# A dilated convolution with a gated activation: another split into six-step and four-step groups, and a new order of all instructions

## The chip, the cores and the metric

The kernel runs on one core of one Trainium2 chip. A core has a matrix engine (PE, with its weight loads PEld), a vector engine (DVE), a scalar engine (ACT), a general engine (POOL, also called GpSimd), a queue engine (SP) and DMA. The engines run side by side, each takes its own instructions strictly in the order in which the program lists them, and they wait for each other by semaphores. The metric is device time in microseconds (us), as a median of several runs.

## The reference: what is computed

`x` has 2 sequences of 16,000 steps with 256 channels; `w` holds three taps of 256 by 512, `w_o` is 256 by 256, all bf16.

```
pad = 4                                  # (K - 1) * dilation, K = 3, dilation 2
xp = pad x with 4 zero steps in front
h = xp[t+4] @ w[0] + xp[t+2] @ w[1] + xp[t] @ w[2]      # B, T, 512
f, g = h[..., :256], h[..., 256:]
z = tanh(f) * sigmoid(g)
return z @ w_o                                           # B, T, 256
```

Three outputs that lie two steps apart share inputs. Done plainly they need nine products of an input by a tap. A fast-convolution scheme of the Toom-Cook kind makes two outputs from four products, or three outputs from five, at the price of sums ahead of the products (over inputs and over weights) and sums behind them (over products).

## The kernel before, in words

**Groups.** The steps of a sequence are cut into groups, named in `GROUPS` (lines 13 to 16). A group of kind A covers `6*R` steps and a group of kind B covers `4*R`; R is 256 unless the word says otherwise. A group of kind P (one, at the very start, `P160`) does the plain three-tap convolution. Channels lie across the 128 partitions and R runs along the free axis, so one product of a group is, for one block of 128 of the 512 outputs, two matmuls (two halves of the 256 input channels) with 2R columns. Before there are 15 groups A, 7 groups B with R = 256, one B160 and one B128.

**Products.** A group has four blocks (`oi` 0 to 3). A block of A has five products, called "first", "mid", "last", "zero" and "inf" (`product`, line 336; tokens F, M, L, Z, I); a block of B has four (no "mid"). They add up in PSUM banks `b` (three buffers) and `a` (two buffers).

**Operands of the products** (`pre` and `operand`, lines 261 to 333). B needs `m`, `p`, `d0`, `d3`, each one sum of two slices of the transposed input `xt`. A needs `u1`, three scaled copies of it (`u3`, `uh`, `ud`), and four sums `rp`, `rm`, `r0`, `ri`, each made out of an `f`, `e`, `u0` or `u2` plus one of those scaled copies. The engine is written in the token: a plain name (`u0.4`) is one DVE instruction over 1,024 elements; a name with `q` (`u0.4q7`) is one of four quarters on POOL, held until the DVE instruction so many places back has finished; a name ending in `d` (`r0.4d`) is an accumulating DMA that POOL issues.

**Behind the products.** Per block: `c` copies bank `b` to `ss` (ACT, line 382); `A` makes the bank `a` start value (DVE, line 388); in A-groups `h` or `k` makes `hh` on DVE or by a copy on ACT (lines 397 and 395) and `Y` makes `yy` (DVE, lines 412 and 414). Then `b`, `y`, `a` are activations on ACT (line 433), three to a block of A and two to a block of B. When two blocks are there, `g` multiplies tanh by sigmoid on DVE (`gate`, line 452), over 1,536 elements for A, 1,024 for B. `P` multiplies 128 rows of z by `w_o` (four matmuls of 256 columns for a pair of steps), `e` or `v` evicts the result to `osb` on ACT or DVE (lines 487 and 479), and `s` stores it from SP (line 496). Loads (`x`) are transposing DMAs on the same SP queue (line 167). The last group's output products are split into a first half (H) and a second half (R).

**Order.** `ORDER` (lines 17 to 21) gives the order of blocks over the whole kernel: four times the group's number, blocks of different groups possibly interleaved. `PLAN` (lines 22 to 72) is a list of all instructions written out by hand or by a planner; each token is emitted in turn, so PLAN fixes the order on every engine and queue, and which of two engines does an `h`/`k`, an `e`/`v` or an operand. Before, groups 8, 9 and 10 (B) come first, and from then on blocks of a B-group stand between blocks of the A-groups ("1 11 1 1 1 11 2 2 2 11").

**Buffers.** `SLOTS` (line 139) says how many buffers each ring has; `osb`, the evicted outputs, has 3.

Of the kernel before, what the change touches and what calls it, by code (L numbers as in the profile page):

```python
# [26 lines left out]
m.3 L e6 F d3.3 b wa.9q1 s3 P A c x F e7 uh.1 M p.3 I k0 g Z c I e.2 a L ud.1 b P f.1q1 A a L x wa.13q47 e8 F Y
wa.11q35 P c A f.1q18 Z y g M wa.15q20 b Z h1 I b u1.2 F a L x u0.2 c I ud.2 e9 F A f.1q1 a M Y P c P k2 u3.1 s4
u2.1 M e10 rm.1d L u1.3 e11 ri.1d Z k3 A I r0.1d b L u3.2 a Y F f.3q10 y P A c Z uh.2 I f.1q16 Y b L y rm.2d u2.2 F
a I f.2 c Z A P a rp.1 M b P y g Z k4 F g e12 e.3q1 L c I s6 A b x P e.3q38 e14 M Y a F m.4q45 h5 I c e.3q32 v13 Z y  # L30
L d3.4q13 v15 b M m.4q10 A P k6 d3.4q7 F Y a L ri.2d u0.3 c Z y A I b P u3.3 f.3q1 Y L a F e16 rp.2d ud.3 Z g c
r0.2d I p.4 b M a A P k7 F u1.4 Z c uh.3 L g b r0.3d M e17 I d0.4q20 A k8 F s8 P Y x f.3q3 c L v19 a d0.4q61 M y Z A
d3.4q27 I h9 b u0.4q53 P y Y u0.4q90 F a L v20 m.4q26 c I A e.3q75 Z e18 s5 Y L a m.4q61 I b g f.3q61 Z y F A b P y
rm.3d u2.3 P c F rp.3d f.4 a Z u2.4 M rp.4d c P g b ri.3d M k10 u3.4 F e21 h11 L u1.5q1 e22 I A c P u1.5q19 a L Y
e23 P d3.4q44 A y M s10 d0.4q13 Y Z e24 s9 u1.5q2 I x b uh.4 I d0.4q48 e25 h12 Z a F g u1.5q1 b L c P Y u0.4q27 y F
A L a P f.5 c Z y A M b u3.5 I x e.4 k13 Z a F ud.4 uh.5 b L u2.5 I c F g e26 M c u1.6q85 P A k14 P u1.6q8 a Y M
rm.4d e27 L v28 e29 I u0.4q7 A s12 k15 P s11 Z ud.5 a u1.6q10 Y L b P u1.6q96 A e30 Z ri.4d y f.6 I s13 b x F Y P a
d0.5 F c p.5 Z e32 L c u0.5 I b u3.6 M A y P k16 r0.4 F a Z v31 e.6q1 c L g I b r0.5d M e33 e.6q17 A F k17 s14 P
u0.6 c s7 d3.5q2 P s1 a Y L e34 d3.5q60 M A y Z e.6q4 I y Y rp.5d P k18 e.5 I b g Z rm.5d a L b u2.6q120 v35 F a P A
c F d3.5q26 e36 Y P d3.5q39 L c g u2.6q62 Z y A P b M ri.5d m.5 e37 Z rp.6d h19 e38 F y e.7 I c L uh.6 I b g r0.6d M  # L40
a u1.7q26 P a h20 F e39 A P u1.7q79 e40 s16 L Y c u2.6q109 s15 P A x Z e.6q71 e42 Y I u1.7q23 b M v41 y u2.7q41 Z
h21 a F u2.6q63 I b g u1.7q4 L c F a Y L c u2.7q64 P A y P rm.6d uh.7 y M A I k22 v44 Z a u3.7 Z ud.6 b L u0.7 e43
ri.6d P ud.7 b F A e45 I u1.8q83 F c Y s18 P a u1.8q154 x M c g u1.8q133 I y M h23 e46 P a f.7q145 h24 Z L g b P
f.8q159 e47 A L e48 x u2.7q23 F Y I Y u1.8q180 c Z a A f.8q125 P b L u2.7q4 e49 Z s19 A f.8q109 F s17 b u3.8 I r0.7d
c u0.8 Z rm.7d a F e.8 b P u2.8 rm.8d c M y F f.7q117 h25 P c ri.7d M g e50 L y I A p.6q1 k26 M Y a P f.7q192 I h27
y f.7q191 L e51 Z f.8q112 A a L p.6q21 b P Y P e52 rp.7d Y F y f.9q107 A Z c I v54 b Z u1.9q53 e53 P m.6 a F ud.8 L
c e.9q0 P A y P rp.8d e55 g M b I s22 h28 Z x a F uh.8 b u2.9 L c P A e.9q1 e56 F Y M f.9q104 c I h29 e57 u1.9q43 I
a M g p.6q6 a L k30 x Z A P u1.9q84 b Y L e58 f.9q114 I v59 y Z u1.9q98 A a F e.9q4 P b Y P c r0.8d ud.9 s23 F e60
u3.9 ri.8d Z g c L d0.6 b I y A M F uh.9 e.10q65 P h31 c Z g a u1.10q5 L y M A b I u1.10q36 Y P e61 F e62 e.10q32
h32 Z a v63 e.9q32 L c I f.9q200 b A M u1.10q16 a Y P y u1.10q39 F h33 Z rp.9d c g L b rm.9d I Y y L ri.9d a A F P  # L50
e64 f.10 Z c s25 u0.9 P s24 b I A s20 r0.9d e65 F u0.10 y M uh.10 c Z u3.10 a P d3.6 M k34 g I b e.11q87 L e66 h35 F
a P A u1.11q32 c L e67 rp.10d Y P M p.6q105 A e69 Z k36 Y r0.10d P b v68 I u2.10q75 y Z v70 a I g u2.10q30 L s27 b
s26 F A x F u2.10q9 c P Y a u1.11q9 P c L u1.11q19 y Z A e.10q142 e71 I ud.10 P b u1.11q8 v72 M e73 u2.10q29 F h37 y
Z e.10q118 c x I g e.11q73 a L M b Y P k38 rm.10d P A e74 L ri.10d u0.11 a F y Z A u1.12q66 c P Y I b M e75 u2.11 Z
a h39 P b f.11 F e76 L g c rp.11d F I m.7q7 A c L a Y d0.7q34 P e77 m.7q16 M A u1.12q14 e78 I s30 h40 Z p.7q33 x a
ud.11 Z b u2.12 L y P d0.7q0 A b I f.12q23 Y F y d3.7q56 F uh.11 c Z g r0.11d c M s29 y p.7q137 P h41 a M d3.7q22
v79 b I e.11q96 L k42 u1.12q12 F a A L u1.12q16 c Y P p.7q33 I A y e.11q62 Z a Y P b L u3.11 e80 Z g rm.11d F e81
uh.12 P ud.12 c u1.13q106 A P y M ri.11d v83 b I d3.7q10 h43 e82 Z a F e.12 s32 m.7q30 L b s31 P c f.12q57 Y F e84
u1.13q96 A M c I u1.13q53 h44 y P p.7q65 e85 M g u1.13q123 a Z L h45 b I f.12q30 A F a f.12q73 Y L c I A rp.12d y Z
Y a d3.7q72 L I b A Z y uh.13 F b u3.12 Z g c rm.12d I a F u0.12 b M g e86 P r0.12d k46 F m.7q16 v87 P c L u1.14 c  # L60
d0.7q12 M e88 A P d0.7q6 a P ri.12d Y k47 M ud.13 e89 L e.13 k48 u0.13q1 Z s34 A e90 s21 I b x P uh.14 u0.13q18 Y a
L F y g u2.13q1 P y A I c Z f.13q10 e91 Y s28 P u0.13q13 b s33 L Z a f.14 u2.13q8 F b A P c ud.14 Z u3.13 F y g M
rm.13d c I m.8q1 b h49 M e92 F u0.13q1 a h50 s35 L e93 f.13q11 I A c P f.13q23 L e94 Y u2.13q20 M e95 Y Z p.8q9 a
h51 e.14q53 P b I A u2.13q19 e96 L y f.13q26 F s37 Y Z a u0.14q15 I b A P rp.13d c F a rp.14d L c Z ri.13d A I r0.13
b Z y M u3.14 v97 F b e.14q1 a P h52 I u2.14q14 y F c g e.14q54 L e98 P Y c M e99 d3.8q30 A P e.14q96 y M h53 s38 P
u0.14q25 e100 Z k54 g u0.14q6 L a I b A P e101 u2.14q78 Y L a F u0.14q31 y P A I c Y d3.8q1 Z a P v102 b Z g y s39 L
# [570 lines left out]
```

## Time and profile before

| what | value |
|---|---|
| median of 3 runs | 262.25 us (261.99 to 262.55) |
| the profiled execution's own time | 262.04 us |
| its span, first to last instruction | 260.3 us |
| granted PE clock | 0.999 |
| PE, DVE, ACT, POOL busy | 253.9, 242.7, 242.9, 170.8 us |

"Busy" is the union of an engine's instructions in time. Instructions of one engine overlap at their ends: a matmul of 512 columns is shown with 379 ns, but the next one can start much earlier. What an engine needs for one instruction is therefore read from the distance between the starts of two that follow without a wait, and busy time is an upper bound of it.

### The profile page before, as it was taken

The page shows a single profiled execution, that of the slowest core. Times are in us where ns is not written, and L with a number is a line of the kernel's source. Part 1 is how long each engine was busy: PE and PEld are TensorE (multiplying, and loading weights), DVE is VectorE, ACT ScalarE, POOL GpSimd, SP SyncE. Part 2 cuts the span into 40 slices and gives each one's busy share as a digit, 9 for nine tenths or more (in the row PEclk, how much of TensorE's full clock was granted, in tenths as well). Part 3 has the DMA queues.
Part 4 walks back from the last instruction along what each step waited for, and adds up shares of the span by engine and source line. Part 5 has one row for each costly group of instructions (what it writes and reads, how often), then busy time and mean ns, then how long its engine had stood idle before and what let it go on. Part 6 is the DMA issues. An engine that isn't in the chain of part 4 may idle for free.

```text
span 260.3 us, 4591 instructions
## 1 busy us (share of the span) xinstructions
PE 253.9 (98%) x1468; PEld 142.0 (55%) x1468; DVE 242.7 (93%) x398; ACT 242.9 (93%) x490; POOL 170.8 (66%) x248
## 2 busy tenths in 40 slices
...
GB/s 198 187 208 213 243 214 204 225 229 123 202 212 263 227 221 222 170 242 200 255 186 184 229 128 256 218 236 150 207 164 78 165 236 136 159 101 42 123 161 171
DMA packets 83583, 49.38 MB, mean 190 GB/s; under 512 B 69064, under 2 KB 70344, under 8 KB 83560
## 3 DMA queue, kind: packets, MB, share of 16 engines
...
q10 hardware_dynamic: 912, 0.95, 1.1%
...
q14 instruction: 12, 0.10, 0.1%
...
## 4 chain that ended last, share of the span: by engine, by line
PE 79%; DVE 13%; issue 2%; DMA 2%; ACT 2%; ACTq 1%; POOL 1%; DVEq 0%
PE b L351 46%; PE o_ps L470 18%; PE a L351 12%; DVE a L385 4%; DVE zz L452 2%; DVE yy L385 2%; DMA e<-u 2%; DVE u L330 1%; PE b L371 1%; PE a L371 1%; DVE hh L385 1%; DVE uh L328 1%; ACTq L189 1%; POOL wu L233 1%; DVE d L330 1%
## 5 line engine op out<-in xcount | busy, mean ns | idle before, releaser
L470 PE MATMUL o_ps<-wo_sb,zz 128*128 128x256 bf16 x496 | 71.9, 273 | 0.1
L385 DVE SCALAR_TENSOR_TENSOR a<-ss,b 128x512 f32<-128x512 f32 (+1 forms) x96 | 64.0, 668 | 5.8 <-PE b L351 4.5
L470 PEld LDWEIGHTS <-zz 128*128 128x128 bf16 x496 | 48.4, 98 | 26.6 <-DVE zz L452 0.9
L382 ACT COPY ss<-b 128x512 f32<-128x512 f32 (+1 forms) x96 | 56.1, 591 | 5.2 <-PE b L351 4.4
L487 ACT CAST osb<-o_ps 128x512 bf16<-128x512 f32 x96 | 57.6, 617 | 0.9 <-PE o_ps L470 0.4
L351 PEld LDWEIGHTS <-w_sb 128*128 128x128 bf16 x384 | 37.4, 98 | 38.5 <-issue 2.3
L330 POOL TENSOR_TENSOR u<-xt 128x256 bf16<-128x256 bf16 x68 | 50.5, 757 | 6.1 <-PE b L351 4.7
L452 DVE TENSOR_TENSOR zz<-th,sg 128x1536 bf16<-128x1536 bf16 (+2 forms) x50 | 44.6, 893 | 1.2 <-ACT sg L433 1.2
L351 PE MATMUL b<-f,wp_sb 128*128 128x512 bf16 x120 | 35.7, 379 | 0.4 <-DVE hh L385 0.4
L351 PE MATMUL b<-e,wm_sb 128*128 128x512 bf16 x120 | 35.7, 379 | 0.2 <-DMA e<-u 0.2
L351 PE MATMUL b<-u,w_sb 128*128 128x512 bf16 x120 | 35.7, 379 | 0.2 <-DVE yy L385 0.2
L351 PE MATMUL a<-u,w_sb 128*128 128x512 bf16 x120 | 35.5, 379 | 0.1
L351 PE MATMUL b<-u,wa_sb 128*128 128x512 bf16 x120 | 35.5, 379 | 0.0
L433 ACT ACTIVATE sg<-a 128x512 bf16<-128x512 f32 (+2 forms) x48 | 29.3, 610 | 0.9 <-PE a L351 0.7
L433 ACT ACTIVATE th<-b 128x512 bf16<-128x512 f32 (+2 forms) x48 | 28.8, 601 | 1.2 <-PE b L351 0.9
L433 ACT ACTIVATE th<-a 128x512 bf16<-128x512 f32 (+2 forms) x48 | 29.2, 611 | 0.1
L433 ACT ACTIVATE sg<-b 128x512 bf16<-128x512 f32 (+2 forms) x48 | 28.8, 600 | 0.5 <-PE b L351 0.2
L351 PEld LDWEIGHTS <-wp_sb 128*128 128x128 bf16 x192 | 18.8, 98 | 18.2 <-issue 1.7
L330 POOL TENSOR_TENSOR e<-xt 128x256 bf16<-128x256 bf16 x24 | 19.7, 823 | 12.2 <-PE b L351 6.7
L351 PEld LDWEIGHTS <-wm_sb 128*128 128x128 bf16 x192 | 18.6, 98 | 14.9 <-DMA e<-u 0.7
L330 POOL TENSOR_TENSOR f<-xt 128x256 bf16<-128x256 bf16 x28 | 21.5, 773 | 6.4 <-DVE ud L328 2.8
L385 DVE SCALAR_TENSOR_TENSOR hh<-ss,b 128x512 f32<-128x512 f32 x34 | 23.0, 678 | 0.5 <-PE b L351 0.2
...
## 6 DMA issues: line engine op xcount, KB each, us to landing
...
out_dram<-osb SPq DMA_DIRECT2D x17, 256.0 KB, 3.3
f<-u POOLq DMA_DIRECT2D x14, 256.0 KB, 4.2
e<-u POOLq DMA_DIRECT2D x14, 256.0 KB, 4.1
u<-ud POOLq DMA_DIRECT2D x14, 256.0 KB, 5.6
u<-uh POOLq DMA_DIRECT2D x13, 256.0 KB, 4.7
w_sb<-in_w_dram ACTq DMA_DIRECT2D x3, 256.0 KB, 3.7
xt<-in_x_dram SPq DMA_TRANSPOSE x24, 6.6
```

The source lines that it names most:

```text
L189: return nc.scalar.dma_start(out=w_taps[tap][:], in_=w[tap].rearrange("(ct c) d -> c ct d", c=P))
L233: return nc.gpsimd.tensor_tensor(out=dst[:, d], in0=wu_sb[0][ct][:, d], in1=wu_sb[1 + add][ct][:, d], op=ALU.add)
L328: ins = eng.tensor_scalar_mul(o, a, factor)
L330: ins = eng.tensor_tensor(out=o, in0=a, in1=b, op=op)
L351: nc.tensor.matmul(G[bank, oi][:, :2 * R], lhsT=wmat[:, ct, osl], rhs=G[mv][:, :, ct, :R], start=which == "first" and ct == 0, stop=ct == ...
L371: nc.tensor.matmul(G[bank, oi][:, :4 * r].rearrange("p (j r) -> p j r", j=4), lhsT=w_taps[tap][:, ct, osl], rhs=xt[:, j0:j0 + 4, ct, c0 + ...
L382: nc.scalar.copy(out=G["ss", oi][:, :n], in_=G["b", oi][:, :n])
L385: return note(nc.vector.scalar_tensor_tensor(out=out, in0=in0, scalar=scalar, in1=in1, op0=ALU.mult, op1=op))
L433: nc.scalar.activation(out=G[name, dt][:, j:j + 2, :R], in_=G[bank, oi][:, :2 * R].rearrange("p (q r) -> p q r", q=2), func=(ACT.Tanh, ACT ...
L452: note(nc.vector.tensor_tensor(out=G["z"][:, dt, :, :n], in0=G["th", dt][:, :, :n], in1=G["sg", dt][:, :, :n], op=ALU.mult))
L470: nc.tensor.matmul(o_ps[:, q, :], lhsT=z, rhs=wo_sb[:, dt, :], start=dt == 0 and (q == 0 or len(dts) == NT), stop=dt == NT - 1, skip_group ...
L487: copy(out=G["osb", at][:, 2 * jp:2 * jp + 2, :], in_=o_ps[:])
```

## The change

GROUPS becomes 18 groups A, 3 groups B with R = 256 and one B160 (the B128 goes); the P160 stays. ORDER then lists whole groups one after the other: B-groups 9, 10, 11, then A-groups 1 to 8 and 12 to 21, then 22 (B160). The ring `osb` gets 4 buffers. PLAN is another list for these groups. By tokens, before and after:

| token | before | after |
|---|---|---|
| F, L, Z, I (each, blocks) | 96 | 88 |
| M, Y, y (each, blocks of A) | 60 | 72 |
| c, A, a, b (each) | 96 | 88 |
| h on DVE / k on ACT | 34 / 26 | 41 / 31 |
| g over 1,536 / 1,024 / 512 elements | 30 / 14 / 2 | 36 / 6 / 0 |
| v on DVE / e on ACT | 29 / 97 | 22 / 104 |
| P and H (pieces of output products) | 124 + 2 | 123 + 3 |
| u3, uh, ud on DVE (each) | 15 | 18 |
| m, p, d0, d3 on DVE (together) | 24 | 13 |
| u0, u1, u2, e, f on DVE (together) | 45 | 54 |
| rp, rm, r0, ri on DVE (together) | 5 | 4 |
| rp, rm, r0, ri as DMA (together) | 55 | 67 |
| quarters on POOL, beside 16 for weights | 168 | 160 |
| loads x (beside the first four) / stores s | 20 / 49 | 18 / 46 |

```diff
 GROUPS = (
-    "P160 A A A A A A A B B B B B128",
-    "A A A A A A A A B B B B160",
+    "P160 A A A A A A A A B B B",
+    "A A A A A A A A A A B160",
 )
 ORDER = """
-8 8 8 8 9 9 9 9 10 10 10 10 1 11 1 1 1 11 2 2 2 11 2 3 3 11 3 3 4 21 4 4 4 21 5 5 5 21 5 6 6 21 6 6 7 22 7 7 7 22 13
-13 13 22 13 14 14 22 14 14 15 23 15 15 15 23 16 16 16 23 16 17 17 23 17 17 18 24 18 18 18 24 19 19 19 24 19 20 20 24
-20 20 12 12 12 12
+9 9 9 9 10 10 10 10 11 11 11 11 1 1 1 1 2 2 2 2 3 3 3 3 4 4 4 4 5 5 5 5 6 6 6 6 7 7 7 7 8 8 8 8 12 12 12 12 13 13 13
+13 14 14 14 14 15 15 15 15 16 16 16 16 17 17 17 17 18 18 18 18 19 19 19 19 20 20 20 20 21 21 21 21 22 22 22 22
 """
 PLAN = """
-p.0 m.0 d0.0 d3.0 F D c D D G w L d F wa.6q3 A F c p.1 Z c I G b L d3.1 wa.7q1 a L A P wa.0q8 A x F wa.2q9 I d0.1 c
...
-v118 a P e119 Z P e120 P b s46 e121 P g s45 v122 H e123 H R R s47 v124 e125 s48
+d3.0 m.0 d0.0 p.0 F D c G F w D L c wa.4q3 F A wa.7q5 L c wa.2q5 D A I wa.6q2 d Z m.1 a Z p.1 b L b G I wa.14q1 F A
...
+s41 P e117 v118 I a Z v119 a P b g P s42 e120 g P H v121 H e122 R H v123 R s43 R e124 s44 v125 s45
 """
...
-    SLOTS = {"m": 2, ..., "th": 2, "osb": 3, "odd": 3}
+    SLOTS = {"m": 2, ..., "th": 2, "osb": 4, "odd": 3}
```

More of the change, by code (lines that the diff above doesn't have):

```diff
@@ L27 @@
[L27 to L66, printed above, removed]
@@ new lines @@
+F d3.1 c x P a d0.1 Z L u2.0 b I A c F a u1.0 L c Z g wa.3q1 I b A P wa.0q14 e0 x F f.0 a L ud.0 c wa.11q1 Z A P
+wa.8q11 b I g rp.0d L e1 m.2 Z ri.0d e2 a F e.0 b P A I c s0 d3.2 F e3 Z a u3.0 P u1.1 b rm.0d I p.2 c L a ud.1 P A
+e4 F wa.15q1 e5 L u2.1 wa.10q9 s2 Z c x A I wa.5q29 b L d0.2 a F g wa.12q1 I c A Z a wa.1q35 L u0.0 wa.13q25 b Z A I
+b wa.9q14 F uh.0 a I g r0.0d c F f.1 a Z u1.2 P c L b u0.1 M e6 A F k0 s3 P u3.1 c e.1 Z L e.2 b rm.1d I A e7
+u0.2q40 P a F Y ri.1d e8 M uh.1 c Z s4 g r0.1d I k1 x u3.2 M b g L y ud.2 F u0.2q1 k2 A P c P rp.1 u0.2q15 e9 M Y a
@@ new lines @@
+L u1.3q26 h3 e10 Z y I u1.3q24 A L b u0.2q4 Y P a u1.3q2 F Y y Z u1.3q41 A c I b rm.2d uh.2 Z x u2.2 a M b u3.3 F
+ud.3 k4 I f.2 F c g L rp.2d y M c ri.2d A P k5 r0.2d M Y a L k6 f.3 P e11 Z A x y L e.3 I b Y P e12 F g a I e13
+u1.4q47 Z A c P b uh.3 u1.4q44 M Y a P u0.3q56 v14 k7 Z y F rm.3d e.4 L b g P c f.4q48 F y A I c M f.4q57 Y e15 M
+u1.4q69 h8 a Z e16 h9 u0.3q10 L b I f.4q15 A e17 L u1.4q70 Y y F s8 u0.3q48 I a Y Z c u0.3q25 A P y rp.3d u0.4 M b Z
+u2.3 k10 F ud.4 a ri.3d L u2.4 b I r0.3d A c P y F uh.4 Y M a P e18 h11 e.5q40 Z c g L e.5q3 e19 M e20 Y I k12 s9
@@ new lines @@
+f.4q1 P A b L ri.4d g a Z rp.4d y F u3.4 P b A rm.4d P c f.5 r0.4d F e21 Y M y I u1.5 c Z u2.5q30 h13 a I b M uh.5
+u3.5 a L u2.5q1 h14 F e22 e.5q58 A P e23 L u1.6q4 c Y s10 P e24 A u1.6q100 M y Z h15 e.6q28 y I Y b u1.6q105 P L a g
+e.6q45 F e25 Z Y e26 I c u2.5q4 A s11 P b x g M y Z k16 ud.5 F u0.5 a P L c u0.6 I e27 A M b u2.6q79 P x e28 h17
+u1.6q43 F y Y P u2.6q100 a L v29 c r0.5d P g e30 Z rp.5d e31 P Y e.5q70 M b A P y s12 F h18 e32 u2.5q66 I c u3.6 s13
+Z ri.5d a rm.5 x L b f.6 M y I Y e.7q109 F k19 A P a e.6q104 L c uh.6 Z e33 A f.7q65 I b e.6q82 M Y y F e.7q39 h20 a
@@ new lines @@
+Z rm.6d g c I L b u2.7q43 v34 M a F A y u2.6q70 P k21 Y u2.6q15 P e35 L u1.7 u2.7q131 c Z A e36 I b f.7q75 M Y P a
+f.7q77 h22 F y rp.6d Z ud.6 s14 c ud.7 P r0.6d b g L ri.6d y I Y e37 F A a P M c u3.7 Z y h23 e.8q77 M b g I e.8q44
+k24 L e39 v38 F a L e.8q57 Y s15 c P x e.8q16 A P y A e.7q98 M e40 Z e41 f.7q62 h25 I b Y e.7q15 P a F f.8 u2.7q15 y
+L c P Y u0.8q49 e42 M A e43 rm.7d Z uh.7 k26 P rp.7d u0.7 b I u1.8 L e44 r0.7d F a g s17 Z s16 c I u3.8 b P A a M
+u2.8 e45 F ud.8 k27 P u2.7q1 Y P c u1.9 L y u0.8q46 P y A Z e46 ri.7d M Y b I rp.8d g k28 Z rm.8d a F f.9 b L e.9 I
@@ new lines @@
+c F e47 A u2.9q111 M c s18 P Y u0.9q15 e48 x M h29 y u0.8q162 Z h30 a P u0.9q175 b L uh.8 L y g F e49 I Y c
+u1.10q112 P A a u0.8q79 M y A Z u0.9q148 k31 I Y u0.9q23 b I ud.9 y L r0.8d u3.9 F a uh.9 rm.9d Z v50 c P u1.10q190
+A b s19 P e51 x M Y a f.10q177 F h32 e52 Z u1.10q10 P c g u2.9q102 L b M e53 Y P y u2.9q51 A F y I u1.10q130 h33 c Z
+e.10 r0.9d L b ri.8 M a F rp.9 k34 I u1.11q137 A c L a Y u1.11q17 M e54 A u2.9q16 Z k35 P uh.10 f.10q167 b x Y I y F
+ri.9d g a Z c L g I b f.11q155 P e55 A F e56 u2.10 f.10q96 M a s21 P Y c s20 P u1.11q148 h36 y M e57 ud.10 Z u3.10
@@ new lines @@
+k37 L u0.10 rm.10d b I A L u1.11q2 e58 F Y a P y f.10q113 A Z c I u0.11 rp.10d b M Y r0.10d a F h38 ri.10d y Z c I g
+L b M u3.11 y u1.12q1 A F a P Y f.11q76 e59 I h39 c u1.12q54 Z s22 a x e.11 f.11q199 L e60 P A b M u1.12q124 e61 Y P
+y f.11q134 F h40 Z e62 rp.11d uh.11 L c ud.11 I e.12 b M e63 A u2.12q28 P s6 k41 Y F s23 u2.12q205 a L g rm.11d y Z
+c P u2.12q208 A I e64 u0.12 M b u1.12q26 P e65 Y F y r0.11d u2.11 s24 Z k42 P u3.12 ri.11d c uh.12 P f.12 a L b g M
+rp.12d e66 I u1.13q58 v67 F k43 P a A L u1.13q135 c Y P y u2.12q72 M A e68 e.13q221 Z e69 h44 P rm.12d b Y I
@@ new lines @@
+u1.13q42 e70 F v71 a Z g u1.13q162 c s26 L s25 b I A x M y Y F a P u2.13 k45 Z c ud.12 L u3.13 y ri.12d M A b P
+e.13q31 h46 e72 I F e73 Y u0.13q186 L a g e.13q202 Z c P y A M b P e.13q201 Y k47 I r0.12d uh.13 e74 F ud.13 a
+rm.13d L u1.14 s27 Z c f.13 P y A M rp.13d b P y Y u0.13q195 I e75 h48 F a Z f.14 c L u3.14 b I g P e76 u2.14q38 F y
+Y M c u2.14q126 A P e77 M e.14q144 h49 e78 Z s28 h50 u0.13q44 a s7 L x b e.14q40 I A L e79 u0.13q37 Y F a u2.14q265
+P Y c Z e.14q239 y A M ri.13d b ud.14 I g k51 Z r0.13d a F rp.14d e.15 P c L v80 e81 I uh.14 f.15q209 b M A y P
@@ new lines @@
+r0.15d u2.16 e94 L b P A f.17q56 P y F Y y f.17q8 P c h60 e.16q162 Z a g M rp.16d b L e.17q29 e95 h61 I y F A s34
+d0.3q36 L a Y e.16q94 P c I A f.17q3 y M Y a rm.16d Z e96 h62 I b Z g L b F uh.16 e97 Y P r0.16d c F A P c ud.16 M
+u0.17 a ri.16d I e98 h63 M p.3q3 y Z s35 h64 e99 L e.17q10 P b A d3.3q94 L a u2.17q62 Y F e101 f.17q252 P v100 c Z
+u2.17q62 e102 Y I e.17q4 b A M y P e.17q79 h65 a F rm.17d g Z c L y I d3.3q0 A b M p.3q27 Y a P rp.17d F e103 h66 Z
+c uh.17 I g b r0.17d L a M u2.17q13 Y e104 F h67 y P s37 d0.3q61 P y A s36 L c ud.17 p.3q1 P e105 Y Z d3.3q75 y A
```

17 lines of the change are left out of this document (9 added, 8 removed).

## The prediction

> **What bounds the kernel now.** I read the page first (busy time, chain), then the table of 10 us stretches, then the order of time in one stretch, then the groups by form.
>
> ```profile
> PE 253.9 (98%) x1468; PEld 142.0 (55%) x1468; DVE 242.7 (93%) x398; ACT 242.9 (93%) x490; POOL 170.8 (66%) x248
> ...
> PE 79%; DVE 13%; issue 2%; DMA 2%; ACT 2%; ACTq 1%; POOL 1%; DVEq 0%
> ```
> ```profile
> 0.00:10.00 10.00, 9.03 (x68) 5.71 (x69) 5.41 (x8) 6.80 (x14) 0.81 (x8) 1.00 0.87 193
> 10.00:20.00 10.00, 10.00 (x56) 5.31 (x55) 9.08 (x18) 8.17 (x19) 2.13 (x4) 1.00 1.05 197
> 20.00:30.00 10.00, 10.00 (x55) 5.21 (x54) 10.00 (x19) 8.94 (x20) 5.64 (x9) 1.00 1.16 235
> 30.00:40.00 10.00, 9.78 (x54) 5.01 (x52) 9.80 (x18) 9.44 (x20) 5.69 (x9) 1.00 1.10 212
> 40.00:50.00 10.00, 9.98 (x52) 4.97 (x51) 10.00 (x18) 9.80 (x21) 6.08 (x9) 1.00 1.11 208
> 50.00:60.00 10.00, 9.97 (x57) 5.26 (x55) 9.89 (x17) 9.52 (x19) 6.72 (x10) 1.00 0.99 217
> 90.00:100.00 10.00, 10.00 (x58) 5.35 (x57) 9.96 (x17) 10.00 (x22) 5.43 (x8) 1.00 1.12 264
> 240.00:250.00 10.00, 10.00 (x71) 6.84 (x70) 9.57 (x18) 9.55 (x22) 0.00 (x0) 1.00 0.29 111
> 250.00:260.00 10.00, 5.97 (x55) 5.09 (x53) 4.72 (x10) 6.02 (x14) 0.00 (x0) 0.99 0.49 186
> ```
> ```profile
> 59.57 0.68 DVE L385 SCALAR_TENSOR_TENSOR yy<-hh,a 128x512 f32<-128x512 f32 x1
> 59.94 0.59 PE L351 MATMUL b<-u,wa_sb 128*128 128x512 bf16 x2
> 60.17 0.42 DVE L328 TENSOR_SCALAR ud<-u 128x1024 bf16<-128x1024 bf16 x1
> 60.37 0.59 PE L351 MATMUL b<-u,w_sb 128*128 128x512 bf16 x2
> 61.69 0.60 PE L470 MATMUL o_ps<-wo_sb,zz 128*128 128x256 bf16 x4
> 62.13 0.59 PE L351 MATMUL b<-u,wa_sb 128*128 128x512 bf16 x2
> 63.25 0.95 DVE L452 TENSOR_TENSOR zz<-th,sg 128x1536 bf16<-128x1536 bf16 x1
> ```
> ```profile
> 4.84 2.62 PE b L371 x18
> ...
> 253.78 2.20 PE o_ps L470 x20
> 256.00 0.59 ACT osb L487
> ```
>
> The chain runs on PE for 79%. Columns of the stretches: length, then busy us (and instructions) of PE, PEld, DVE, ACT, POOL, then clock, DMA share, GB/s. Since a busy PE says little, I take distances of starts: two matmuls of 512 columns take 0.43 us (59.94 to 60.37), 0.215 each, four of 256 take 0.44 (61.69 to 62.13), 0.11 each. PE's need is 824 matmuls of 512 columns (15 x 40 + 7 x 32), 177.2 us; 80 of 320 columns (B160 and P160) at 0.134 by proportion, 10.8; and 532 of 256 (500 output products, 32 of B128), 58.5. Sum 246.5. From the first real product at 4.84 to the last at 253.78 + 2.20 = 255.98 are 251.1 us. So PE loses only 4.6 us to everything else. PE binds in every stage.
>
> But DVE and ACT are close behind: between 20 and 60 us DVE is busy 39.69 of 40 us, and PE hardly stops.
>
> **The change part by part.** *PE.* Three groups A more (3 x 40 matmuls of 512), four B less (4 x 32), one B128 less (32 of 256): 8 x 0.215 + 32 x 0.11 = 5.2 us less. Output products are 500 in both. That is the gain offered: 3 x 1,536 outputs from 120 matmuls in place of 144 equivalents.
>
> *DVE and ACT.* Their prices:
>
> ```profile
> L385 DVE SCALAR_TENSOR_TENSOR a<-ss,b 128x512 f32<-128x512 f32 x88 | 60.3, 687 | 4.3 <-PE b L351 3.2 <-ACT hh L395 0.3 <-ACT sg L433 0.2
> L487 ACT CAST osb<-o_ps 128x512 bf16<-128x512 f32 x96 | 57.6, 617 | 0.9 <-PE o_ps L470 0.4
> L382 ACT COPY ss<-b 128x512 f32<-128x512 f32 x88 | 53.0, 608 | 4.8 <-PE b L351 3.9 <-ACT th L433 0.2
> L330 POOL TENSOR_TENSOR u<-xt 128x256 bf16<-128x256 bf16 x68 | 50.5, 757 | 6.1 <-PE b L351 4.7 <-DVE yy L385 0.3 <-DVE hh L385 0.2
> L452 DVE TENSOR_TENSOR zz<-th,sg 128x1536 bf16<-128x1536 bf16 x30 | 32.1, 1073 | 0.0
> L433 ACT ACTIVATE th<-a 128x512 bf16<-128x512 f32 x44 | 27.4, 626 | 0.1
> L433 ACT ACTIVATE sg<-yy 128x512 bf16<-128x512 f32 x30 | 19.6, 653 | 0.3 <-DVE yy L385 0.2
> L330 DVE TENSOR_TENSOR u<-xt 128x1024 bf16<-128x1024 bf16 x28 | 19.3, 701 | 0.0
> L479 DVE CAST osb<-o_ps 128x512 bf16<-128x512 f32 x28 | 18.7, 680 | 0.2 <-PE o_ps L470 0.2
> L351 PEld LDWEIGHTS <-wm_sb 128*128 128x128 bf16 x192 | 18.6, 98 | 14.9 <-DMA e<-u 0.7 <-ACT ss L382 0.6 <-issue 0.2
> L325 POOL DMA_DIRECT2D u<-ud x14 | 16.1, 1148 | 2.0 <-DVE ud L328 2.0
> L452 DVE TENSOR_TENSOR zz<-th,sg 128x1024 bf16<-128x1024 bf16 x14 | 10.0, 711 | 0.0
> L328 DVE TENSOR_SCALAR uh<-u 128x1024 bf16<-128x1024 bf16 x15 | 7.5, 500 | 0.0
> L328 DVE TENSOR_SCALAR ud<-u 128x1024 bf16<-128x1024 bf16 x15 | 6.6, 437 | 0.0
> L328 DVE TENSOR_SCALAR u<-u 128x1024 bf16<-128x1024 bf16 x15 | 6.5, 431 | 0.0
> L385 DVE SCALAR_TENSOR_TENSOR a<-ss,b 128x256 f32<-128x256 f32 x4 | 1.7, 425 | 0.4 <-PE b L351 0.3
> ```
>
> DVE loses 4 full `a` sums (4 x 0.687 = 2.75) and 4 half-wide (4 x 0.425 = 1.70), 8 gates of 1,024 (x 0.711 = 5.69) and 2 of 512 (some 0.4 each, 0.8), 7 evictions (x 0.680 = 4.76), and of the operand sums 13 (11 of m, p, d0, d3, one of them half-wide, and 2 of r0; 0.701 each, 8.8): 24.5 us. It gains 7 `hh` and 12 `yy` (same instruction as the `a` sum, 19 x 0.687 = 13.05), 6 gates of 1,536 (x 1.073 = 6.44), 10 operand sums (4 u1, 1 u0, 1 e, 3 f, 1 rp; 7.0) and 3 each of uh, ud, u3 (3 x 1.368 = 4.10): 30.6 us. Net +6.1 us.
> ACT loses 4 `ss` copies (2.43) and 4 half-wide (0.62 of the full price by the two `a` rows, 1.51), 8 full activations (5.0) and 8 half-wide (3.1): 12.0. It gains 12 activations of `yy` (7.84), 5 `hh` copies (3.04), 7 evictions (4.32): 15.2. Net +3.2 us. So ACT stands at 246.1 busy, DVE at 248.8.
>
> *What of this is on the path.* PE alone would end 5.2 us earlier: span 260.3 - 5.2 = 255.1. DVE has to fit. In the first 20 us it is busy 5.41 + 9.08 = 14.5, in the last 20.3 us 9.57 + 4.72 = 14.3; start and tail keep their shape. Between them lie 220 us with 242.7 - 28.8 = 213.9 busy, 6.1 idle. After: 213.9 + 6.1 = 220.0 us busy in a middle that PE would like to be 214.8 long. By busy time DVE becomes the bound: 40.3 + 220.0 = 260.3, no gain at all. But busy time overstates: the `yy` of 59.57 lasts 0.68 and is followed at 60.17, so an instruction needs 0.08 less than it shows wherever it is followed at once. Nothing in the profile separates overlapped tails from true need, so bounds: below, 0.08 comes off each of the 398 instructions, whose durations, from the first row of this table (60.3) to the smallest, sum to 270.1: need 238.3; above, the 242.7 themselves. Less its ends, the middle needs 209 to 213.9 now and 215 to 220 after, without a single wait.
> DVE's waits: now 6.1 us; in the stage 20 to 60, where DVE sets the pace, 0.31 of 40 (0.8%), 1.7 us over the middle. With the latter the upper need gives 40.3 + 220.0 + 1.7 = 262.0. The other end is PE's 255.1. Neither row is nearer; I take the middle, 258.5: the gain of 5.2 is offered, some 3.4 is given back to DVE and ACT, which are both full from 20 us on, where before B blocks between A blocks gave them rest.
>
> One rule of the skill speaks against the change. Row first: a gate of 1,536 took 0.95 us at 63.25 and 1.073 in the mean, and `uh` 0.500 where `u3` of the same shape took 0.431. The Trainium skill, "SBUF — State Buffer", section "Who interferes with whom", says that a DVE instruction with two SBUF inputs and a GpSimd one that reads SBUF exclude each other for the whole instruction. The trace agrees in kind. By that rule six more gates and three more `uh` at 0.12 and 0.07 would be 0.9 us, and the sum 0.9 later, were the mean prices above not to hold it already.
>
> *POOL.* 8 quarters fewer (8 x 0.757 = 6.1) and 12 accumulating DMAs more (12 x 1.148 = 13.8 at the dearest row): +7.7, 178 of about 259 us, off the path; behind each stand the next operand's quarters, which are wanted several us later. Lower end 0, upper end 7.7 if POOL were the bound, which its 66% excludes; I take 0.
> *SP.* Two loads and three stores fewer on the queue, the same bytes: 0. The fourth `osb` buffer: evictions wait only for PE (row L487, 0.9 us in all), so it brings 0 to 0.9, I take 0.
> *Start.* B-groups first, as before, and the same 16 weight quarters: 0, within 1 us either way.
> *Tail.* The last group is B160 in place of B128: activations, gate and one more half-wide eviction. Between 0 and 1.2 us (two more instructions of about 0.6, row 256.00); I take 0.3.
>
> Sum: span 258.5 + 0.3 = 258.8; 1.74 around it (262.04 own time against 260.3) gives 260.5 against 262.04; the median before stands 0.2 above that run: about 260.6. I forecast 260.5, 0.7% faster.
>
> **The rivals.**
> *PE stays the bound.* For it: 20 to 60 us, DVE 99% busy and PE not stopping. Against it: there ACT was at 94%, now both are full. Time: 255.1 + 0.3 + 1.95 = 257.4.
> *DVE and ACT pass their waits on (slower).* Place: the long run of A-groups from about 30 to 225 us, with no B block between. Engines that take instructions in order cannot catch up once all three are full; each wait of DVE for bank `b` (3.2 us on the `a` row) then lengthens the kernel. At the upper need with today's 6.1 us of waits: 40.3 + 220.0 + 6.1 + 0.3 + 1.95 = 268.7; at the lower need 263.7. It decides once need and waits of the middle exceed 220.3 us: then the time is above 262.8.
> *Late DMAs (slower).* Each A-group hangs on its four accumulating DMAs. They grow from 55 to 67 and lie denser:
>
> ```profile
> u<-ud POOLq DMA_DIRECT2D x14, 256.0 KB, 5.6
> ```
> An A-group moves 0.79 MB in, 0.79 out and 4 x 0.26 by accumulation, 2.6 MB in some 11.5 us: 229 GB/s, against 264 carried at 90 to 100 us. So it should fit. If it doesn't, PE waits as it did once for `e` (0.7 us in all, PEld row): 0.3 to 0.7 us in each of 18 groups, 263 to 270.
>
> **How the numbers follow.** A change under 0.2% (0.5 us) can't be told from none. PE stays the bound, about 257.4: 0.15. Gain partly given back, 258 to 261.7 with 260.5 the likeliest: 0.40. Given back wholly, 261.7 to 262.8: 0.12. Waits passed on, 263 to 268: 0.25. Late DMAs: 0.08. So faster 0.55, same 0.12, slower 0.33. The range reaches from PE's floor, 257.0, to 265.0, which leaves out the upper part of the two slow cases; the likeliest one's own range is 257.4 to 262.
>
> **What would show it.** Right: 1,428 matmuls; DVE busy near 248 and ACT near 246 with the span at 258 to 259; stretches from 30 to 220 us with DVE and ACT both at 9.9 or more; DVE's and ACT's share of the chain far above 13% and 2%. PE then shows less than 10.00 in many stretches. PE's rival: PE's share of the chain stays near 80%. The slow rival: DVE's waits for `b` or for ACT stay at 6 us or grow. The DMA rival: PE or PEld waits on `e`, `f` or `u` by DMA, and landings well above 5.6 us. The prediction is wrong most easily where the need of DVE for an instruction differs from my middle of two bounds, or where POOL's and DVE's exclusion grows in the dense stage.

## The result, and the profile after

| kernel | median (range), executions | ratio to the kernel before, with its 95% interval |
|---|---|---|
| before, first series | 262.19 us (261.99 to 262.55) | 1 |
| after, first series | 259.94 us (259.83 to 263.96), 4 | 0.9907 (0.9893 to 0.9921) |
| before, second series | 262.33 us (261.57 to 262.99), 24 | 1 |
| after, second series (the first experiment) | 260.45 us (259.7 to 265.3), 12 | 0.9945 (0.9914 to 0.9976) |

The ratios compare mean times and leave out executions more than 1.5% above the fastest of the same kernel, so for a kernel that scatters they differ from the ratios of the medians. The changed kernel is faster by 0.5 to 0.9%; 260.5 us was forecast. But its executions fall into two groups, which those of the kernel before do not: 7 of 12 took 259.7 to 260.8 us and 5 took 262.4 to 265.3. Both profiles taken of it are of long ones (263.96 and 263.39 us), so I read them for what lengthens these, and read the short ones from a kernel that differs only in the place of one load ("load later", below; 259.82 us, span 258.0).

Engine row and three stretches of the profile after (columns as before):

```profile
PE 251.0 (96%) x1428; PEld 138.6 (53%) x1428; DVE 244.4 (93%) x404; ACT 244.1 (93%) x490; POOL 179.1 (68%) x252
```
```profile
60.00:70.00 10.00, 7.70 (x42) 3.75 (x41) 7.63 (x14) 7.89 (x16) 6.22 (x10) 1.00 1.24 155
...
150.00:160.00 10.00, 10.00 (x59) 5.48 (x57) 10.00 (x17) 10.00 (x22) 9.39 (x13) 1.00 1.11 236
...
190.00:200.00 10.00, 8.62 (x48) 4.41 (x46) 9.91 (x15) 8.86 (x18) 7.50 (x11) 1.00 1.06 218
```

All 40 matmuls are gone (1,428). At 150 us PE, DVE and ACT are all three busy for the whole stretch. PE loses most of its time in two places: from 60 us on, where all engines are idle for part of the stretch (for want of a DMA, as the next rows show), and at 190 to 200 us, where DVE stays busy and PE waits for it. The waits of the same profile, with total, count and longest:

```profile
PE b L351 <- DMA u<-uh: 2.1, 2, 1.9
...
PEld L351 <- DMA f<-u: 1.6, 2, 0.9
...
PE b L351 <- DVE hh L385: 1.3, 2, 1.2
```

Below, "gaps" is one number for a whole profile: the distances between the starts of successive matmuls less the time of their columns (0.215 us for 512, 0.11 for 256), added up over all matmuls from 4 us on. It is 4.5 us before, 10.6 in the profile after.

### The profile page after: what moved, and what is told of

It is laid out like the page before. It is cut to its first block, busy times and chain, and to the rows that moved or that the text cites. A ratio compares the mean times of both kernels' runs of the same rounds, so it can differ in the third digit from the quotient of the medians.

```text
span 262.1 us, 4570 instructions
## 1 busy us (share of the span) xinstructions
PE 251.0 (96%) x1428; PEld 138.6 (53%) x1428; DVE 244.4 (93%) x404; ACT 244.1 (93%) x490; POOL 179.1 (68%) x252
## 4 chain that ended last, share of the span: by engine, by line
PE 53%; DVE 9%; issue 3%; ACT 1%; DVEq 0%
PE b L351 32%; PE o_ps L470 13%; PE a L351 8%; DVE a L385 2%; DVE yy L385 2%; DVE zz L452 1%; DVE hh L385 1%; DVE osb L479 1%; DVE f L330 1%; DVE u L330 1%; ACT th L433 0%; DVE ud L328 0%; DVE uh L328 0%; DVE u L328 0%; ACT ss L382 0%
## 5 line engine op out<-in xcount | busy, mean ns | idle before, releaser
L330 POOL TENSOR_TENSOR u<-xt 128x256 bf16<-128x256 bf16 x84 | 62.4, 757 | 15.2 <-PE a L351 5.3
L351 PE MATMUL b<-u,w_sb 128*128 128x512 bf16 x144 | 42.8, 379 | 2.7 <-DMA u<-uh 2.1
L351 PE MATMUL b<-f,wp_sb 128*128 128x512 bf16 x144 | 42.7, 379 | 2.2 <-DVE hh L385 1.3
L351 PE MATMUL b<-u,wa_sb 128*128 128x512 bf16 x144 | 42.8, 379 | 0.0
L351 PE MATMUL b<-e,wm_sb 128*128 128x512 bf16 x144 | 42.7, 379 | 0.0
L433 ACT ACTIVATE th<-b 128x512 bf16<-128x512 f32 (+1 forms) x44 | 28.0, 637 | 2.3 <-PE b L351 2.0
L433 ACT ACTIVATE sg<-b 128x512 bf16<-128x512 f32 (+1 forms) x44 | 28.0, 636 | 1.5 <-PE b L351 1.4
L433 ACT ACTIVATE sg<-a 128x512 bf16<-128x512 f32 (+1 forms) x44 | 27.7, 631 | 0.8 <-PE a L351 0.7
L433 ACT ACTIVATE th<-a 128x512 bf16<-128x512 f32 (+1 forms) x44 | 28.1, 639 | 0.1
L385 DVE SCALAR_TENSOR_TENSOR yy<-hh,b 128x512 f32<-128x512 f32 x41 | 27.6, 678 | 0.5 <-PE b L351 0.3
```

Source lines behind the costliest of these rows:

```text
L330: ins = eng.tensor_tensor(out=o, in0=a, in1=b, op=op)
L351: nc.tensor.matmul(G[bank, oi][:, :2 * R], lhsT=wmat[:, ct, osl], rhs=G[mv][:, :, ct, :R], start=which == "first" and ct == 0, stop=ct == ...
L385: return note(nc.vector.scalar_tensor_tensor(out=out, in0=in0, scalar=scalar, in1=in1, op0=ALU.mult, op1=op))
L433: nc.scalar.activation(out=G[name, dt][:, j:j + 2, :R], in_=G[bank, oi][:, :2 * R].rearrange("p (q r) -> p q r", q=2), func=(ACT.Tanh, ACT ...
```

## The experiments

**The changed kernel again.** No edit.

> The changed kernel once more, unaltered, for an undisturbed profile. Theory A (three engines full: PE, DVE and ACT share the loss): 259.9 us, PE's matmul starts show 6 to 7.5 us of gaps between 5 us and the end, most of them behind DVE or ACT, DVE busy near 248. Theory B (PE alone is still the bound and the missing 2.9 us of the 5.2 are lost to late accumulating DMAs): 259.9 us, PE or its weight loads wait 2 us or more on e, f or u by DMA.

Measured: the second series of the table. In its order of time (start, length, what, and in brackets what was waited for), the load at 47.71 us and the DMAs behind it:

```profile
47.71 20.12 SPq L167 DMA_TRANSPOSE xt<-in_x_dram  x2
...
49.24 0.86 POOL L325 DMA_DIRECT2D f<-u  x1 [2.09 <-DVE f L330]
49.78 1.21 POOL L325 DMA_DIRECT2D u<-ud  x1
50.31 1.56 POOL L325 DMA_DIRECT2D u<-uh  x1
...
63.89 0.59 PE L351 MATMUL b<-u,w_sb 128*128 128x512 bf16 x2 [1.50 <-DMA u<-uh]
```
Two of its stretches of 2.5 us:
```profile
52.50:55.00 2.50, 2.50 (x17) 1.47 (x16) 2.50 (x5) 2.50 (x7) 1.09 (x1) 1.00 1.36 119
...
62.50:65.00 2.50, 1.11 (x8) 0.74 (x9) 2.50 (x6) 1.33 (x3) 1.42 (x3) 1.00 1.26 84
```
and its DMA groups from 45 to 70 us (the last number is the median from issue to landing):
```profile
u<-uh POOLq DMA_DIRECT2D x2, 256.0 KB, 12.0
...
xt<-in_x_dram SPq DMA_TRANSPOSE x3, 13.4
```

The two loads shown as one row of 20.12 us are the second and third of three in a row. The third begins at 53.0 us, some 3 us behind three accumulating DMAs, and takes 14.8 us on its queue. Meanwhile the DMA share, which adds up the packets' times, is 1.36 and 1.26 in these two stretches and so no lower than the 1.23 and 1.08 of the 5 us ahead of the first, but the engines move 119 and 84 GB/s where they moved 259 and 218. The accumulation issued at 50.31 is there for PE at 63.89. In the kernel before, the three loads of this window landed after a median of 6.7 us, its accumulations after 3.7 to 5.6. The granted clock was 1.0 in this execution, so the clock is not what made it long. Both profiled long executions of the changed kernel (263.96 and 263.39 us) lose their time to late DMAs; the short ones are still to be explained.

**More work for each engine, after and before.** Six kernels with one more instruction in each A-group, at its second block (18 groups after, 15 before). For DVE one sum of 144 elements behind the `a` sum, written to a corner that is not used again; for ACT one copy of 200 elements; for PE the first matmul of "first" done twice, which changes the values of that product.

```diff
             stt(G["a", oi][:, :n], ss, 3.0 if G["kind"] == "A" else -2.0, b)
+            if G["kind"] == "A" and oi == 1:
+                nc.vector.scalar_tensor_tensor(out=xns[1][:, 0, :144],
+                    in0=G["ss", oi][:, :144], scalar=3.0, in1=G["b", oi][:, :144], op0=ALU.mult, op1=ALU.add)
```
```diff
+        if G["kind"] == "A" and oi == 1:
+            nc.scalar.copy(out=xns[1][:, 0, :200], in_=G["b", oi][:, :200])
```
```diff
-        for ct in range(CT):
+        for ct in ((0, 0, 1) if which == "first" and oi == 1 and G["kind"] == "A" else range(CT)):
```

> The changed kernel with one more DVE sum of 144 elements (about 0.215 us) per six-step group, 18 in all, 3.9 us of DVE work that nobody reads. Theory A (DVE is full): 2 to 3.9 us more than the changed kernel, 262 to 263.8. Theory B (PE alone bounds, DVE has slack): under 1 us more, 259.9 to 260.9.

> The changed kernel with one more ACT copy of 200 elements (about 0.21 us) per six-step group, 18 in all, 3.8 us of ACT work that nobody reads. Theory A (ACT is full too): 2 to 3.8 us more than the changed kernel, 262 to 263.7. A with DVE alone as the second bound: under 1 us more. Theory B: under 1 us more.

> The changed kernel with one matmul of 512 columns (0.215 us) done twice per six-step group, 18 in all, 3.9 us more of PE work. Theory A (PE stands behind DVE and ACT part of the time): 1 to 3 us more, 261 to 263. Theory B (PE alone bounds): the full 3.9 us, 263.8.

> The kernel before with the same extra DVE sum of 144 elements in each of its 15 six-step groups, 3.2 us of DVE work. Both theories have PE as the only bound before the change: under 1 us more, 262.2 to 263.2. If it costs 2 us or more, DVE was a bound before as well, and theory A does not say why the change gave something back.

> The kernel before with the same extra ACT copy of 200 elements in each of its 15 six-step groups, 3.2 us of ACT work. Both theories: under 1 us more, 262.2 to 263.2.

> The kernel before with one matmul of 512 columns done twice in each of its 15 six-step groups, 3.2 us of PE work. Both theories: nearly the full price, 2.7 to 3.2 us more, 264.9 to 265.4.

| engine | added, after | time after, median (range) | ratio | added, before | time before, median (range) | ratio | cost before |
|---|---|---|---|---|---|---|---|
| DVE | 3.9 us | 263.53 (262.92 to 263.94) | 1.0049 (1.0031 to 1.0067) | 3.2 us | 265.38 (265.08 to 265.94) | 1.0116 (1.0101 to 1.0132) | 3.0 us |
| ACT | 3.8 us | 265.22 (261.5 to 287.3) | 1.0043 (1.0009 to 1.0076) | 3.2 us | 263.49 (262.89 to 263.76) | 1.0039 (1.0027 to 1.0051) | 1.1 us |
| PE | 3.9 us | 269.56 (266.36 to 273.24) | 1.0233 (1.019 to 1.0276) | 3.2 us | 264.74 (264.3 to 265.2) | 1.009 (1.0077 to 1.0104) | 2.4 us |

The ratios are to the unaltered kernel before. In the kernel before nothing scatters, and the last column reads straight: DVE's instruction cost nearly its full price, where under 1 us was expected. So it was wrong that PE alone bound the kernel before. Which part of this is DVE's time can't be told: the sum reads bank `b` and so also holds it 0.2 us longer. PE's own addition cost only 2.4 of 3.2, and its gaps fell from 4.5 to 3.6 us: a quarter of it went into waits that were there anyway.

After, DVE's addition costs 3.6 of 3.9 us against the 259.9 of the short executions, about the same share as before. It removes the late DMAs, too: the third load took 6.6 us there, though its place in the list is the same, and its executions do not scatter (262.92 to 263.94). With more work for ACT or PE the DMAs are late again, in the same stretch and in others (with more work for PE a load issued at 51.2 us landed after 20.0); ACT's fastest five are 1.6 to 4.0 us above 259.9, the rest up to 27. In the profile with more work for PE:

```profile
PEld L351 <- DMA f<-u: 1.7, 1, 1.7
...
PE b L351 <- DMA f<-u: 1.4, 1, 1.4
```
Its fastest execution is 6.5 us above 259.9, of which 3.9 are the matmuls; in its profile most of the rest stands as waits for DMAs, of which these two rows show one, seen from the weight load and from the matmul. For ACT and PE the cost of the time alone is therefore not separated.

**A cheaper gate.** If DVE's need took part of the gain, it should come back with 14 us less of DVE work. The gate becomes a product with a constant, leaving tanh out of the result:

```diff
-        note(nc.vector.tensor_tensor(
-            out=G["z"][:, dt, :, :n], in0=G["th", dt][:, :, :n], in1=G["sg", dt][:, :, :n], op=ALU.mult
-        ))
+        note(nc.vector.tensor_scalar_mul(G["z"][:, dt, :, :n], G["sg", dt][:, :, :n], 0.5))
```

> The changed kernel with the gate cut down: DVE scales sigmoid's half by 0.5 instead of multiplying tanh by sigmoid (the product by tanh is left out, so this part of the computation is not done). Per gate of 1,536 elements that should take 0.4 us less of DVE, some 17 us in all. Theory A with DVE as the main second bound: 1.5 to 2.9 us less, down to PE's floor of 257.1 to 258.4. Theory A with ACT as the main second bound, or theory B: 0 to 1 us less, 258.9 to 259.9.

Measured: 263.96 us (259.85 to 277.08, 12 executions), ratio 0.9984 (0.9953 to 1.0015). Its engine row, and the longest of PE's waits:

```profile
PE 249.0 (95%) x1428; PEld 138.6 (53%) x1428; DVE 230.0 (88%) x404; ACT 242.8 (93%) x490; POOL 174.3 (67%) x252
```
```profile
PE b L351 <- DMA u<-uh: 5.8, 2, 3.7
```
DVE has 14 us less to do and the kernel gains nothing: the fastest execution equals those after (259.85 against 259.7), the others are 1 to 17 us longer, in the profile for want of DMAs: one accumulation issued at 39.9 us landed after 15.0. That the DMAs are late because a faster DVE lets them be issued at other times is argued, not shown.

**The third load later.** The load moves some 40 tokens down the list and is held by a DVE gate, so that it no longer follows the three accumulations:

```diff
-... P e11 Z A x y L e.3 I b Y P e12 F g a I e13
+... P e11 Z A y L e.3 I b Y P e12 F g a I e13
-... v14 k7 Z y F rm.3d e.4 L b g P c f.4q48 F ...
+... v14 k7 Z y F rm.3d e.4 L b g X P c f.4q48 F ...
+        elif what == "X":
+            load(next(to_load), behind=made_v[-1])
```

> The changed kernel with one load moved: the third of three loads that stand in a row on SP's queue at 40 to 68 us (the one issued at 53.0 in the changed kernel's profile, 3 us behind three accumulating DMAs) waits for a DVE gate that ends about 57 us. Theory C (in part of its executions the changed kernel loses 2 to 5 us because this load and the accumulating DMAs ahead of it land late, 13 to 20 us after issue): the executions above 262 us go, all lie at 259.6 to 260.3, and no landing of a load is above 12 us. Theory D (the scatter has another source): executions between 262 and 265 us remain, as 5 of 12 did.

Measured: 260.08 us (259.82 to 260.13, and one execution of 264.4; 6), ratio 0.9916 (0.9899 to 0.9933). Minimum, median and longest landing of accumulations (line 325) and loads (line 167), first in the repeated kernel, then in this one:

```profile
DMA to landing us min/median/max: 3.3/5.4/13.4
...
DMA to landing us min/median/max: 4.4/7.5/19.6
```
```profile
DMA to landing us min/median/max: 3.3/5.3/8.2
...
DMA to landing us min/median/max: 4.5/7.6/10.4
```

The medians stay, the long landings are gone, and with them the waits for DMAs between 60 and 80 us. That fits theory C but does not show it, for three reasons. This profile is of a short execution, and no short one of the unmoved kernel was profiled. With the load at its old place 9 of 28 executions took over 262 us (1 of 4, 5 of 12, and 3 of 12 with three output buffers, below), here 1 of 6 and in the next experiment none of 8, both on another chip than the two series of 12: a hint, but no proof. And the first load of the three, issued at about 39.8 us in both and ahead of the one that was moved, already landed after 11.4 us in the repeated kernel and after 8.8 here, so the two executions differ before the edit can act. The one execution of 264.4 has no profile and stays unexplained. The short executions are as short as before: 260.1 us is about what the unaltered kernel takes when its DMAs are in time.

This profile is the undisturbed one. Engine row and chain:

```profile
PE 249.5 (97%) x1428; PEld 138.3 (54%) x1428; DVE 243.6 (94%) x404; ACT 243.5 (94%) x490; POOL 178.8 (69%) x252
...
PE 54%; DVE 9%; issue 2%; ACT 2%; DVEq 0%; ACTq 0%
```
Its stretches, the ends, the middle and the one bad place:
```profile
0.00:10.00 10.00, 9.02 (x66) 5.65 (x67) 5.22 (x8) 6.61 (x14) 0.81 (x8) 1.00 0.84 191
10.00:20.00 10.00, 10.00 (x56) 5.22 (x54) 8.78 (x18) 8.34 (x18) 2.33 (x5) 1.00 1.05 193
...
60.00:70.00 10.00, 10.00 (x55) 5.21 (x54) 9.84 (x17) 10.00 (x22) 8.52 (x13) 1.00 1.01 220
...
180.00:190.00 10.00, 9.32 (x53) 4.75 (x52) 10.00 (x16) 9.71 (x20) 8.40 (x12) 1.00 1.11 175
190.00:200.00 10.00, 9.28 (x54) 5.11 (x53) 9.81 (x16) 9.18 (x19) 6.54 (x11) 1.00 1.12 264
...
240.00:250.00 10.00, 10.00 (x73) 7.05 (x72) 8.56 (x15) 9.26 (x22) 0.00 (x0) 1.00 0.27 100
250.00:260.00 10.00, 2.59 (x24) 2.06 (x21) 3.10 (x8) 2.42 (x6) 0.00 (x0) 0.84 0.37 138
```

From 20 to 240 us DVE is busy 243.64 - (5.22 + 8.78 + 8.56 + 3.10) = 218.0 of 220 us, and PE hardly stops except around 190. The order of time there:

```profile
189.13 0.59 PE L351 MATMUL b<-u,w_sb 128*128 128x512 bf16 x2 [0.68 <-DVE yy L385]
...
190.18 0.95 POOL L330 TENSOR_TENSOR u<-xt 128x256 bf16<-128x256 bf16 x1
190.18 1.78 DVE L452 TENSOR_TENSOR zz<-th,sg 128x1536 bf16<-128x1536 bf16 x1
...
192.62 0.59 PE L351 MATMUL b<-f,wp_sb 128*128 128x512 bf16 x2 [0.72 <-DVE hh L385]
```

A gate of 1,536 elements takes 1.78 us instead of about 0.95, because a quarter `u<-xt` on POOL starts in the same instant, as the next experiment shows. PE loses 0.84 us before and 0.89 us behind it (from matmul starts). The first loss ends at 189.13, a microsecond ahead of the gate, so the gate can't have made it, and it is not a wait for `yy` either, though the row says so: in the repeated kernel the same matmul starts before that `yy` does.

```profile
191.89 0.59 PE L351 MATMUL b<-u,w_sb 128*128 128x512 bf16 x2
...
191.99 0.67 DVE L385 SCALAR_TENSOR_TENSOR yy<-hh,a 128x512 f32<-128x512 f32 x1
```

In the next experiment it waits for the accumulation `u<-uh` and starts 0.14 us behind its landing. Here that accumulation, issued at 181.49, lands at 189.00, 0.13 us ahead of the matmul: the first loss is most likely a late DMA.

**The POOL quarter held as well.** In PLAN the quarter `u2.15q180` becomes `u2.15q0`: it waits for the gate just issued.

```diff
-... P e84 s29 u2.15q180 P h54 ...
+... P e84 s29 u2.15q0 P h54 ...
```

> The same, and one quarter of a sum on POOL (the one at 193.8 us) is held until the DVE gate that starts at the same moment has finished. Theory E (POOL's read of SBUF stops DVE's gate: it took 1.78 us there against 0.95 at other places, and PE then waited 1.3 us): the gate takes 0.95 to 1.05 us, PE's gap at about 196 us shrinks from 1.3 to under 0.6 us, and the time is 0.7 to 1.2 us below that of the kernel with the load moved, 258.6 to 259.3. Theory F (that gate is late for its own reasons): no change within 0.3 us.

Measured: 261.16 us (258.92 to 261.54, 8 executions), ratio 0.9944 (0.992 to 0.9968). In its order of time:

```profile
190.88 0.94 DVE L452 TENSOR_TENSOR zz<-th,sg 128x1536 bf16<-128x1536 bf16 x1
...
192.48 0.59 PE L351 MATMUL b<-f,wp_sb 128*128 128x512 bf16 x2 [0.33 <-DVE hh L385]
...
208.78 0.60 PE L351 MATMUL b<-e,wm_sb 128*128 128x512 bf16 x2 [0.99 <-DMA e<-u]
```

The gate is back at 0.94 us: POOL's instruction was the cause. PE's gap behind it falls from 0.89 to 0.50 us, and the two gaps of this place together from 1.73 to 0.89, by about what the gate was stretched (0.83). So the mechanism is that of theory E, but the time that it named, 258.6 to 259.3, was missed: PE waits at 208.78 for an accumulation that is issued no later than with the quarter not held (198.96 against 199.09) and lands after 9.8 us instead of 5.6, and 0.7 of the 1.5 us by which this profile is longer are lost before 190 us, where the two instruction lists are the same. There, too, the accumulations issued at 48.8 to 49.9 landed after 9.6 to 11.0 us, against 8.2 at most with the load moved alone. So DMAs are late in some executions with the load moved as well, and the median does not show what holding the quarter is worth. One execution, 258.92, is 0.9 us under the best with the load moved; it has no profile.

**Cheaper gate with the load moved.** The two edits together, to see DVE's need without the known late load.

> The kernel with the load moved (260.08 us) and the gate cut down: DVE scales sigmoid's half by 0.5, tanh's half is left out of the product. DVE has some 13 us less to do, and the collision of the load with the accumulating DMAs is out of the way. Theory A (DVE's need gives the gain back): 257.0 to 258.6, DVE's waits grow by what it no longer does, PE's gaps fall from 6.4 us to 3 to 5. Theory G (the loss is in the order: waits between single instructions and late DMAs, not in DVE's total): within 0.7 us of 260.1, or slower where earlier DVE work makes POOL and DMAs collide elsewhere.

Measured: 264.15 us (259.11 to 281.39, 12 executions), ratio 0.997 (0.9934 to 1.0005). Its engine row and two of its waits:

```profile
PE 251.2 (94%) x1428; PEld 139.0 (52%) x1428; DVE 230.1 (86%) x404; ACT 243.2 (91%) x490; POOL 174.3 (65%) x252
```
```profile
PE b L351 <- DMA e<-u: 5.9, 2, 3.0
...
PEld L351 <- DMA u<-uh: 3.5, 1, 3.5
```

Again PE waits for DMAs, in three places (gaps of 3.4, 3.0 and 3.2 us at about 54, 108 and 216 us), the first of them that of the cheaper gate above. The fastest execution is 0.7 us below the fastest with the load alone moved (259.82). That is the most that 13.5 us less of DVE work brought in any execution; with DMAs in time throughout it might be more, which no run shows. So 3.9 us more of DVE work cost 3.6 us, and 13.5 us less brought at most 0.7. That fits a second bound close behind DVE, but the sum's longer hold on bank `b` and the late DMAs leave room for other readings.

**Three output buffers.** SLOTS `osb` from 4 back to 3.

```diff
-    SLOTS = {"m": 2, ..., "osb": 4, "odd": 3}
+    SLOTS = {"m": 2, ..., "osb": 3, "odd": 3}
```

> The changed kernel with three output buffers, as before the change: the fourth undone. If the fourth buffer brings nothing (evictions waited only for PE): 259.7 to 260.5 in the undisturbed executions. If it is needed by the new order, in which stores stand later behind loads on SP's queue: evictions wait for stores, 1 us or more slower.

Measured: 260.44 us (259.86 to 265.53, 12 executions, 9 of them up to 261.3), ratio 0.9942 (0.9914 to 0.997). With four buffers it was 260.45 and 0.9945. The fourth buffer makes no difference that can be measured.

No variant beats the changed kernel's short executions reliably. The one with the load moved has their time, and one long execution in six.

## Why the prediction was right, and where only its number was

The time came out as the likeliest case gave it, and the mechanism that this case named is mostly not what happened. That it came so close is partly luck: the forecast gave back 1.5 us too much in waits and put the tail 0.8 us too short, and the median of 260.45 lies between two kinds of execution, near 259.9 and above 262. Against the profile before, span by span, the undisturbed one (of the kernel with the load moved) has:

| term | forecast | measured |
|---|---|---|
| PE's own work | -5.2 us | -5.2 us (1,428 matmuls) |
| given back in waits of PE | +3.4 us | +1.9 us (gaps 4.5 to 6.4), about as much as the 1.7 lost at 189 to 193 us |
| tail | +0.3 us | +1.07 us |
| span | -1.5 us | -2.3 us (260.27 to 257.96) |

**PE's gain: right.** All 5.2 us.

**"Some 3.4 is given back to DVE and ACT, which are both full": this step failed.** They are full, as forecast: DVE 218.0 of 220 us. But full engines cost PE little: outside one place the gaps grew by 0.2 us. Of the 1.7 us at that place about half (0.84, by the experiment that held the POOL quarter) comes from one gate of nearly double length beside a POOL instruction, and not from DVE's need; the other half stays with the quarter held. In its small waits this is nearest to the rival that PE stays the bound, but PE is not alone: the small DVE sum cost over 0.9 of its own time before and after. The rule that I had weighed under the mean prices, the Trainium skill, "SBUF — State Buffer", section "Who interferes with whom", speaks of just this exclusion of a DVE instruction with two SBUF inputs and a GpSimd one that reads SBUF; the trace agrees, with 1.78 us beside POOL and 0.94 with POOL held. I had spread it as 0.12 us over all gates, and had set `uh` beside it, which has one input and is no case of it. In the trace 7 of 36 gates take over 1.15 us (9 of 30 before), and the one of 1.78 came at a moment when PE had nothing in store.

**DVE's price: too high, as a busy time.** Forecast were +6.1 us and 248.8; it is +0.9, 243.6. Added durations rose only from 270.1 us (398 instructions) to about 273.5 (404), because prices fell in the new mix, and the union grew less still, most likely since tails overlap more in a dense stage. Two groups by form of the profile after, against 1,073 and 500 ns before:

```profile
L452 DVE TENSOR_TENSOR zz<-th,sg 128x1536 bf16<-128x1536 bf16 x36 | 37.5, 1045 | 0.0
...
L328 DVE TENSOR_SCALAR uh<-u 128x1024 bf16<-128x1024 bf16 x18 | 8.7, 483 | 0.0
```

This points to a need near my lower bound, not in the middle; the need itself was not measured. ACT: +3.2 forecast, +0.6 measured (243.5). The signs that I had named for the likeliest case split accordingly: DVE and ACT full in the stretches came true in part (both at 9.9 or more in 8 of the 19 stretches from 30 to 220 us, DVE never under 9.7), their share of the chain did not (DVE 9% and ACT 2%; the chain breaks off at 67%, so this weighs little).

**"PE binds in every stage" before: too simple.** A DVE sum of 0.2 us in each A-group cost 94% of itself in the kernel before. The profile before shows how little PE stops, and I read that as slack of the others. It only shows that they kept pace. (How much of the 94% is the longer hold on bank `b` stays open, as said above.)

**The tail: mis-sized.** The last matmuls and what follows, in the profile with the load moved, and the last store of the profile before:

```profile
251.78 0.82 PE L470 MATMUL o_ps<-wo_sb,zz 128*128 128x256 bf16 x6
...
252.63 0.69 DVE L479 CAST osb<-o_ps 128x512 bf16<-128x512 f32 x1 [0.22 <-PE o_ps L470]
...
253.38 0.34 SPq L496 DMA_DIRECT2D out_dram<-osb  x1
```
```profile
255.74 1.21 SPq L496 DMA_DIRECT2D out_dram<-osb  x2
```
From the last matmul's start to the end of the span are 5.64 us instead of 4.57. Of the 1.07, 0.1 lie ahead of the end of the last store's issue, and from there to the end of the span it takes 257.96 - 253.72 = 4.2 us, before 260.27 - 256.95 = 3.3. Most of this difference is not the store either: by its semaphore it lands 2.5 us after that in place of 2.3, and from the landing to the end of the span, where only semaphore and drain instructions run, it is 1.7 us in place of 1.0. That is no chance of one profile, for the whole tail is 5.6 us in every profile with the new groups and 4.6 in every one with the old. I had counted instructions (activation, gate, eviction) and nothing behind them; why the program's end takes longer was not looked into.

**Late DMAs: a chance of 0.08 for something that lengthens 5 of 12 executions.** They lift the median by some 0.5 us, and I reasoned from the mean (229 GB/s wanted, 264 carried) and took the landings to stay near their median. The medians rose by little (5.4 us for accumulations, 4.3 before). The longest landing did not: 8.8 before, 13.4 to 14.1 after.

**At nothing, and rightly:** the fourth buffer (260.44 against 260.45), the start (first matmul at 0.77 to 0.78 us in all profiles), and POOL's own time, 178.8 us busy as forecast (178). Its instructions are not quite beside the work, though: one of them lengthened that gate.

Open stays how much DVE's and ACT's need alone costs after the change, since PE waited for late DMAs in the profiles of all kernels that relieved DVE, and what makes the DMAs late.
